# Zeros in the 11 unused columns of the values' stationary operand

## The chip, the core and the metric

The kernel runs on one core of one Trainium2 chip. The core has TensorE (PE in the profile; the loads of its stationary operand are listed apart as PEld), VectorE (DVE), ScalarE (ACT), GpSimd (POOL) and SyncE (SP), which mostly issues DMAs. The metric is the device time of one execution in microseconds, the median of several runs. About 0.2% (3.6 us) is what runs of this kernel can tell from no change.

## The reference

A gated sum of two branches over the same x of 2048 tokens by 640 channels, all in float32: 32-head attention with 20 channels a head, and a token-mixing MLP whose hidden width is 1728.

```python
def _A_ref(x, wqkv, wo):
    qkv = (lambda x, *d: x.transpose(*d))((x @ wqkv).reshape(B, S, 3, H, Dh), 2, 0, 3, 1, 4)
    q, k, v = qkv[0], qkv[1], qkv[2]
    scores = jnp.einsum("bhqd,bhkd->bhqk", q, k) * (Dh ** -0.5)
    p = _softmax(scores, axis=-1)
    o = jnp.einsum("bhqk,bhkd->bhqd", p, v)
    return (lambda x, *d: x.transpose(*d))(o, 0, 2, 1, 3).reshape(B, S, D) @ wo

def _B_ref(x, w1, b1, w2, b2):
    h = _layernorm(x, axis=-1)                                  # (B, S, D)
    u = _gelu(jnp.einsum("bsd,sf->bdf", h, w1) + b1)            # (B, D, F)
    y = jnp.einsum("bdf,fs->bds", u, w2) + b2                   # (B, D, S)
    return (lambda x, *d: x.transpose(*d))(y, 0, 2, 1)

g = _sigmoid((x * gate_w).sum(-1, keepdims=True))
return g * _A_ref(x, wqkv, wo) + (1 - g) * _B_ref(x, w1, b1, w2, b2)
```

(The reference's shapes: S = 2048, D = 640, H = 32, Dh = 20, F = 1728. The steps of gelu are written in one line here.)

## The kernel before

**Stages.** The program goes through these in order: the projections to queries and keys (`qk`, line 55), in the middle of them the projection to values (`v`, also line 55, called from lines 434 to 461); the MLP (`u` and `y`, line 49), with a first part of the score maxima (`s`, line 212) mixed in; the attention loop; and the output projection (`a`, line 1122). Products that must be exact to float32 are split into a high and a low part of the faster float32r type and done in three passes.

**The values.** For each half of the heads (16 heads) and each of the 16 token tiles t, 15 matmuls fill one PSUM tile with 128 tokens by 320 values. A POOL memset (line 454) writes ones in column 20 of each head in an SBUF tile `vt`, an ACT copy (line 455) brings the 320 values beside them, 21 columns a head, and one DMA on SP's queue (line 456) stores `vt` in the DRAM tensor `v_d`. `vt` has three buffers; the PSUM tiles of this stage go round four. In the second half of the heads ACT also squares a tile of x for the layer norm's statistics after each copy (line 432), and POOL issues the DMA that loads the tile of x four steps ahead (line 428). There the order of ACT, DVE and PE is as written; POOL's and SP's is set by the framework's scheduler up to the end of this stage, and as written behind it.

**The attention loop.** 16 pairs p of heads, and for each pair 32 iterations: two halves qh of 1024 queries by 16 tiles kt of 128 keys. One iteration g does:

- `st_pair` (line 1015): two matmuls of 512 queries, one a head, in the upper and lower 64 rows of the array, into the two banks of the PSUM tile `two`, which has a single buffer; then one ACT exponential of 1024 columns (line 1020) into an SBUF tile `pp` (three buffers).
- `st_one` (line 1023), twice: one matmul of 512 queries, then one ACT exponential of 512 columns (line 1028) into an SBUF tile `pt` (six buffers).
- between these, two matmuls `s` (line 212) for the score maxima of a later pair, each reduced by DVE (line 218); they run out 23 iterations before the end of the loop, where matmuls of the output projection of the first token tile take their place in most iterations.
- `pv_flush` (line 911): for the iteration before, four products of exponentials and values, one for each of two heads and two groups of 512 queries, in float32. Each fills 32 columns of the array (`pv[r: r + 32]`, r = 0, 32, 64, 96). The stationary operand is 32 columns of the values' tile `v`, of which 21 belong to the head: 20 values and the column of ones, whose result is the softmax's denominator.

In the profile each of the four `pv` products shows as two matmuls and two weight loads. Every 16 iterations the result is copied to SBUF (`pv_evac`, line 888) and stored.

**Where the 32 columns lie.** `v` holds for each key tile the 42 columns of a pair of heads, 21 and 21. Head 0 takes columns 0 to 31, so that its last 11 are the first 11 of head 1; head 1 takes columns 10 to 41, so that its first 11 are the last 11 of head 0. The results in those 22 rows of PSUM are never read: `pv_evac` picks rows `r` to `r + 20` for head 0, and 11 further for head 1. `load_v` (line 160) loads one pair's `v` from `v_d` while the pair before is worked on (iteration 13 of 32, line 1067); `v` has two buffers in the pool `base`. The first pair's is loaded in eight pieces during the MLP (line 814).

**Waits.** The framework gives each engine a semaphore and puts the waits into the instruction. An instruction that has to wait for two semaphores gets a separate semaphore instruction ahead of it in its engine's queue.

## Time and profile before

| what | value |
|---|---|
| time, median of 3 runs | 1786.04 us (1785.62 to 1786.98) |
| profiled execution | span 1786.8 us; the page gives no other time of its own for it |
| PE busy | 99% of the span, 15000 matmuls |
| ACT busy | 83% |
| DVE, POOL busy | 69%, 37% |
| the values' stage | 70.9 us, from 67.1 to 138.1 |
| the attention loop | 735 to 1708 us, 511 iterations with an exponential each and one whose exponentials are done before the loop |

A row of a timeline has the start and the duration in us, the engine, the line of the code, the operation, what it writes and reads, how many instructions were merged, and in brackets how long the engine had been idle before and what ended that. A busy PE is no PE at its peak, since the profile models the ends of pipelined matmuls: the share of 99% does not by itself say that PE sets the pace.

### The profile page before, as it was taken

What the parts mean: (1) busy time and instruction counts of PE and PEld (TensorE: products, weight loads), DVE (VectorE), ACT (ScalarE), POOL (GpSimd) and SP (SyncE); (2) the same over time, 40 slices, a digit from 0 to 9 for tenths busy, and PEclk for the clock granted to TensorE, in tenths of its full rate; (3) what the DMA queues carried; (4) which work ended last, traced back from release to release, by engine and by line L of the source; (5) the groups of instructions that cost most, each with busy time, mean ns of one, the idle gap of its engine ahead of it and who ended that gap; (6) DMA issues with size and microseconds to landing.
All of it is one profiled execution on the core that took longest, in us unless ns stands there. A gap on an engine that the chain in (4) does not pass through costs nothing.

```text
span 1786.8 us, 39925 instructions
## 1 busy us (share of the span) xinstructions
PE 1774.7 (99%) x15000; PEld 1106.2 (62%) x15000; DVE 1227.1 (69%) x2380; ACT 1483.3 (83%) x2534; POOL 654.3 (37%) x925
## 2 busy tenths in 40 slices
PE   9999999999999999999999999999999999999999
PEld 7998899999999999633333333333333333333378
DVE  5303288888888889776767676776777677767245
ACT  4244388888888886799999999999999999999930
POOL 1123578789877777211211111121322121212200
PEclk9999999999999999999999999999999999999999
DMA  8757876466675564335313224043353242301543
GB/s 280 251 167 241 268 182 167 142 182 200 176 191 146 160 173 150 82 72 119 63 31 86 54 64 96 10 110 66 49 136 70 46 94 57 74 13 47 195 132 134
DMA packets 155516, 222.34 MB, mean 124 GB/s; under 512 B 66420, under 2 KB 93444, under 8 KB 151640
## 3 DMA queue, kind: packets, MB, share of 16 engines
q1 hardware_dynamic: 136698, 188.82, 38.9%
q0 software_dynamic: 15888, 25.76, 6.0%
q10 hardware_dynamic: 2736, 5.21, 1.1%
q8 instruction: 118, 1.93, 0.5%
q14 instruction: 76, 0.62, 0.1%
HBM read 165.43 MB, written 53.92 MB: 123 GB/s over the span
## 4 chain that ended last, share of the span: by engine, by line
PE 96%; DMA 3%; DVE 0%; issue 0%; ACT 0%; POOL 0%; SPq 0%; DVEq 0%; ACTq 0%; POOLq 0%
PE pv L917 29%; PE st L1013 20%; PE s L212 13%; PE u L49 10%; PE y L49 10%; PE qk L55 7%; PE v L55 4%; PE a L1122 3%; DMA xr<-in_xT_dram 1%; DMA wr<-in_wqk_dram 1%; DMA rc_d<-rl_last 1%; DMA rbe<-r_d 0%; PE a L49 0%; DMA o_d<-oev 0%; DVE mx L218 0%
## 5 line engine op out<-in xcount | busy, mean ns | idle before, releaser
L218 DVE TENSOR_REDUCE mx<-s 128x1 f32<-128x512 f32 x1280 | 835.2, 687 | 285.7 <-PE s L212 214.3
L1028 ACT ACTIVATE p<-st 128x512 f32<-128x512 f32 x1022 | 567.5, 627 | 0.0
L917 PE MATMUL pv<-p,v 128*32 128x512 f32 x4088 | 546.8, 605 | 0.0
L1020 ACT ACTIVATE p<-st 128x1024 f32<-128x1024 f32 x511 | 536.8, 1051 | 2.6 <-PE s L212 1.8
L1013 PEld LDWEIGHTS st<-qs_True,ks_True 62*128 62x128 f32 x2044 | 245.3, 185 | 430.9 <-ACT p L1020 426.9
L1013 PE MATMUL st<-qs_True,ks_True 62*128 62x512 f32 x2044 | 495.5, 445 | 0.4 <-DVE ty L697 0.4
L212 PE MATMUL s<-ks_False,qs_False 60*128 60x512 f32 x1152 | 361.1, 394 | 0.1
L44 POOL TENSOR_TENSOR wl<-wr,wh 128x512 fp32r<-128x512 f32 x228 | 275.8, 1221 | 65.2 <-ACT wh L41 48.0
L237 DVE CUSTOM_DVE_ANT_0 ov<-s,ov 128x512 f32<-128x512 f32 x384 | 264.0, 688 | 38.0 <-PE s L212 25.9
L227 ACT ACTIVATE ov<-s 128x512 f32<-128x512 f32 x384 | 229.0, 598 | 65.1 <-PE s L212 54.6
L212 PE MATMUL s<-sk,sq 60*128 60x512 f32 x896 | 280.6, 394 | 0.0
L49 PE MATMUL y<-gh,wh 64*128 64x320 f32 x896 | 224.3, 307 | 0.0
L49 PE MATMUL y<-gl,wh 64*128 64x320 f32 x832 | 216.2, 306 | 0.0
L49 PE MATMUL y<-gh,wl 64*128 64x320 f32 x832 | 215.8, 305 | 0.0
L898 POOL DMA_DIRECT2D l_d<-oev x124 | 60.8, 497 | 410.4 <-DVE oev L890 402.1
L49 PE MATMUL u<-hh,wh 64*128 64x320 f32 x864 | 199.9, 307 | 0.0
L49 PE MATMUL u<-hl,wh 64*128 64x320 f32 x864 | 199.8, 307 | 0.0
L212 PEld LDWEIGHTS s<-ks_False,qs_False 60*128 60x128 f32 x1152 | 198.0, 185 | 2.4 <-DVE mx L218 0.4
L917 PEld LDWEIGHTS pv<-p,v 128*32 128x32 f32 x4088 | 82.3, 108 | 182.9 <-issue 169.9
L49 PE MATMUL u<-hh,wl 64*128 64x320 f32 x800 | 188.2, 307 | 0.0
L41 ACT ACTIVATE wh<-wr 128x512 fp32r<-128x512 f32 (+3 forms) x247 | 146.8, 598 | 37.7 <-PE y L49 13.3
L212 PEld LDWEIGHTS s<-sk,sq 60*128 60x128 f32 x896 | 166.1, 186 | 18.1 <-DVE mx L218 0.4
(148 smaller groups left out, 2388.2 us busy)
## 6 DMA issues: line engine op xcount, KB each, us to landing
wr<-in_w_dram SPq DMA_DIRECT2D x192, 256.0 KB
ks_True<-k_d SPq DMA_DIRECT2D x96, 160.0 KB
qs_True<-q_d SPq DMA_DIRECT2D x192, 80.0 KB
qs_False<-q_d SPq DMA_DIRECT2D x96, 80.0 KB
sk<-k_d SPq DMA_DIRECT2D x42, 160.0 KB
sq<-q_d SPq DMA_DIRECT2D x84, 80.0 KB
v_d<-vt SPq DMA_DIRECT2D x32, 168.0 KB
xr<-in_xT_dram SPq DMA_DIRECT2D x20, 256.0 KB
```

The lines of the kernel that those rows point to most:

```text
L41: nc.scalar.activation(hi, src, AF.Copy)
L44: (lo_eng or nc.vector).tensor_sub(lo, src, hi.bitcast(F32))
L49: nc.tensor.matmul(ps[k], a[r], b[r], start=start, stop=stop)
L55: nc.tensor.matmul(ps, a, b, start=(i == 0 and k == 0), stop=(i == n - 1 and k == 2))
L212: nc.tensor.matmul(ps, qs[half][r, t * P:(t + 1) * P], ks[r, kc * 512:(kc + 1) * 512], start=True, stop=True)
L218: nc.vector.tensor_reduce(mx[:, slot, j, t: t + 1], ps, axis=AX.X, op=OP.max)
L227: nc.scalar.activation(over[j, kc], ps, AF.Relu)
L237: nc.vector.tensor_tensor_reduce(ov, ps, ov, 1.0, -3.0e38, OP.add, OP.max, mx[:, slot, j, t: t + 1])
L917: nc.tensor.matmul(pv[r: r + 32, :], v_tiles[p][:, kt, 10 * j: 10 * j + 32], pt[j, c], start=(kt == 0), stop=(kt == NT - 1))
L1013: nc.tensor.matmul(ps, ks[r, kt * P:(kt + 1) * P], qs[qh][r, c * 512:(c + 1) * 512], start=True, stop=True)
L1020: nc.scalar.activation(pt, ps, AF.Exp, scale=SCALE)
L1028: nc.scalar.activation(pt, ps, AF.Exp, scale=SCALE)
```

## The change

The tile `v` becomes 53 columns wide for a pair of heads: 21 of head 0, 11 columns of zeros, 21 of head 1. Head 0 takes columns 0 to 31 as before (its 21, then the zeros), head 1 columns 21 to 52 (the zeros, then its 21), so that each head's results lie in the same rows of PSUM as before, and the 22 rows that are never read become zeros. In full:

```diff
-NPAIR = VW * 2
+NPAIR = 32 + VW
...
-    v_d = dram.tile([2, NT, P, 16 * VW], F32, name="v_d")
+    v_d = dram.tile([2, NT, P, 8 * NPAIR], F32, name="v_d")
...
     def load_v(p, pieces=1, put=nc.sync.dma_start):
-        v_tiles[p] = base.tile([P, NT, NPAIR], F32, tag="v", bufs=2, name=f"v{p}")
+        v_tiles[p] = (ap if p % 2 else base).tile([P, NT, NPAIR], F32, tag="v", bufs=1, name=f"v{p}")
         c0 = NPAIR * (p % 8)
...
-            vt = pvp.tile([P, 16, VW], F32, tag="vt", bufs=3, name=f"vt{half}_{t}")
-            nc.gpsimd.memset(vt[:, :, DH], 1.0)
-            nc.scalar.activation(vt[:, :, :DH], ps[:, :HALF].rearrange("p (h w) -> p h w", w=DH), AF.Copy)
+            vt = pvp.tile([P, 8, NPAIR], F32, tag="vt", bufs=3, name=f"vt{half}_{t}")
+            nc.gpsimd.memset(vt[:, :, VW: 32], 0.0)
+            for j in range(2):
+                nc.gpsimd.memset(vt[:, :, 32 * j + DH], 1.0)
+                nc.scalar.activation(vt[:, :, 32 * j: 32 * j + DH], ps[:, :HALF].rearrange("p (h j w) -> p h j w", j=2, w=DH)[:, :, j], AF.Copy)
             nc.sync.dma_start(v_d[half, t], vt.rearrange("p h w -> p (h w)"))
...
-                    nc.tensor.matmul(pv[r: r + 32, :], v_tiles[p][:, kt, 10 * j: 10 * j + 32], pt[j, c],
+                    nc.tensor.matmul(pv[r: r + 32, :], v_tiles[p][:, kt, VW * j: VW * j + 32], pt[j, c],
                                      start=(kt == 0), stop=(kt == NT - 1))
...
-        pt = lp.tile([P, 512], F32, tag="pt", bufs=6, name=f"p{g}_1{j}")
+        pt = lp.tile([P, 512], F32, tag="pt", bufs=5, name=f"p{g}_1{j}")
```

So for each of the 32 tiles `vt`, three memsets stand in place of one and two ACT copies of 160 values in place of one of 320; a store has 212 KB in place of 168, and a load of `v` 424 KB in place of 336. The two buffers of `v` now lie in two pools, `base` for even and `ap` for odd pairs, and `pt` has five buffers in place of six.

The waits move too, which the diff does not show. The first place is ACT in the attention loop, iterations 37 and 38. In a row, `p37_0` is the exponential of `st_pair`, `p37_10` and `p37_11` those of the two `st_one`; the brackets name the semaphores that are waited for (`PE_49` is PE's, `Activation_49` ACT's own). Before:

```order
L1020 ACTIVATE p37_0_14441<-st37_0_14438 128x1024 [waits PE_49,Activation_49]
L1028 ACTIVATE p37_10_14445<-st37_10_14443 128x512 [waits PE_49,Activation_49]
L1028 ACTIVATE p37_11_14455<-st37_11_14453 128x512 [waits PE_49]
L1020 ACTIVATE p38_0_14487<-st38_0_14484 128x1024 [waits PE_49,Activation_49]
L1028 ACTIVATE p38_10_14491<-st38_10_14489 128x512 [waits PE_49,Activation_49]
L1028 ACTIVATE p38_11_14501<-st38_11_14499 128x512 [waits PE_49]
```

And with the change:

```order
L1022 ACTIVATE p37_0_14537<-st37_0_14534 128x1024 [waits PE_49]
L1030 ACTIVATE p37_10_14541<-st37_10_14539 128x512 [waits PE_49,Activation_49]
L1030 ACTIVATE p37_11_14551<-st37_11_14549 128x512 [waits PE_49]
L1022 ACTIVATE p38_0_14583<-st38_0_14580 128x1024 [waits PE_49]
L1030 ACTIVATE p38_10_14587<-st38_10_14585 128x512 [waits PE_49,Activation_49]
L1030 ACTIVATE p38_11_14597<-st38_11_14595 128x512 [waits PE_49]
```

The wide exponential no longer waits for ACT's own semaphore, so that it needs no semaphore instruction ahead of it; this is so in 508 of the 511 iterations. PE's order in the loop and its waits are as before.

The second place is POOL in the second half of the values' stage, tiles 3 to 6 (`vt1_3` and so on; `xn` are the tiles of x; `DMAHW` waits are for the store that frees the buffer). Before:

```order
L454 MEMSET vt1_3_1150 128x16 [waits DMAHW2_49,Pool_49]
L428 DMA xn5_1109<-in_x_dram 128x640 [waits DMASW1_49,Activation_49]
L454 MEMSET vt1_4_1173 128x16 [waits DMAHW3_49,Pool_49]
L428 DMA xn6_1132<-in_x_dram 128x640 [waits DMASW2_49,Activation_49]
L454 MEMSET vt1_5_1196 128x16 [waits DMAHW4_49,Pool_49]
```

And with the change:

```order
L428 DMA xn5_1163<-in_x_dram 128x640 [waits DMASW1_49,Activation_49]
L454 MEMSET vt1_4_1233 128x8x11 [waits DMAHW3_49,Pool_49]
L456 MEMSET vt1_4_1233 128x8 x2
L428 DMA xn6_1189<-in_x_dram 128x640 [waits DMASW2_49,Activation_49]
L454 MEMSET vt1_5_1259 128x8x11 [waits DMAHW4_49,Pool_49]
L456 MEMSET vt1_5_1259 128x8 x2
```

Each memset has become three, at the same place between the DMAs. Beside this, 12 of the second half's 16 value tiles and the four `qk` tiles behind them get a second wait on their first matmul, for PE's own semaphore, and so do DVE's 16 small copies of the gate's columns (line 458), so that PE and DVE each have 16 semaphore instructions more. PE's waits are for a matmul three tiles back.

## The prediction

> **What bounds the kernel now.** I read the chain of waits first, then the clock by stage, then single iterations of the attention loop. The chain's shares and its three longest pieces:
>
> ```profile
> PE pv L917 29%; PE st L1013 20%; PE s L212 13%; PE u L49 10%; PE y L49 10%; PE qk L55 7%; PE v L55 4%; PE a L1122 3%; DMA xr<-in_xT_dram 1%; DMA wr<-in_wqk_dram 1%; DMA rc_d<-rl_last 1%; DMA rbe<-r_d 0%; PE a L49 0%; DMA o_d<-oev 0%; DVE mx L218 0%
> ...
> 34.00 33.13 PE qk L55 x137
> 67.13 70.92 PE v L55 x480
> 138.05 84.00 PE qk L55 x360
> ```
>
> The chain is PE nearly throughout. The change touches two stages: the values' stage, 480 matmuls without a break in 70.92 us, and the attention loop, whose `pv`, `st` and `s` are 62% of the chain. PE's modelled ends would hide a wait, so the loop has to be checked by starts. First its pace, as the wide exponential, one an iteration, shows it in the part with the `s` matmuls (738 to 1663 us) and in the part after they have run out; the columns are the stretch, its length, ACT's busy time in this line with the count, the granted TensorE clock, the DMA share and GB/s:
>
> ```profile
> 738.00:1663.00 925.00, 508.92 (x487) 1.00 0.32 69
> 1663.00:1707.00 44.00, 26.42 (x23) 1.00 0.57 196
> ```
>
> 925.00 / 487 = 1.899 us an iteration with `s`, 44.00 / 23 = 1.913 without. PE has less to do in the second part and is not faster: there something else sets the pace. Two stretches of the timeline, one of each part (start, duration, in brackets the idle time ahead):
>
> ```profile
> 1041.85 1.04 ACT L1020 ACTIVATE p<-st 128x1024 f32<-128x1024 f32 x1
> 1042.15 1.07 PE L917 MATMUL pv<-p,v 128*32 128x512 f32 x8
> 1042.77 1.09 ACT L1028 ACTIVATE p<-st 128x512 f32<-128x512 f32 x2
> 1043.14 0.29 PEld L1013 LDWEIGHTS st<-qs_True,ks_True 62*128 62x128 f32 x3 [0.84 <-ACT p L1020]
> 1043.74 1.04 ACT L1020 ACTIVATE p<-st 128x1024 f32<-128x1024 f32 x1
> 1044.04 1.07 PE L917 MATMUL pv<-p,v 128*32 128x512 f32 x8
> 1045.04 0.29 PEld L1013 LDWEIGHTS st<-qs_True,ks_True 62*128 62x128 f32 x3 [0.84 <-ACT p L1020]
> 1045.64 1.04 ACT L1020 ACTIVATE p<-st 128x1024 f32<-128x1024 f32 x1
> ```
>
> ```profile
> 1665.24 1.05 ACT L1020 ACTIVATE p<-st 128x1024 f32<-128x1024 f32 x1
> 1665.37 1.11 PE L917 MATMUL pv<-p,v 128*32 128x512 f32 x8
> 1666.41 0.19 PEld L1013 LDWEIGHTS st<-qs_True,ks_True 62*128 62x128 f32 x2 [0.84 <-ACT p L1020]
> 1667.11 1.09 ACT L1020 ACTIVATE p<-st 128x1024 f32<-128x1024 f32 x1
> 1668.31 0.19 PEld L1013 LDWEIGHTS st<-qs_True,ks_True 62*128 62x128 f32 x2 [0.84 <-ACT p L1020]
> 1668.96 1.13 ACT L1020 ACTIVATE p<-st 128x1024 f32<-128x1024 f32 x1
> ```
>
> The next `st` may load only when the wide exponential has emptied the single PSUM tile `two`. Without `s` the exponential ends at 1667.11 + 1.09 = 1668.20 and the load follows at 1668.31, 0.11 later: ACT comes last. With `s` it ends at 1043.74 + 1.04 = 1044.78 and the load comes at 1045.04, 0.26 later. If 0.11 is enough, 0.15 us of ACT's lead goes unused and PE comes last, whatever the bracket names: the load follows the eight `pv` matmuls after 0.99 (1042.15 to 1043.14) and 1.00 us (1044.04 to 1045.04).
>
> ACT is close behind. Without `s` the wide exponentials start 1.87 and 1.85 us apart (1665.24, 1667.11, 1668.96), but their durations grow from 1.05 to 1.13, so that they end at 1666.29, 1668.20 and 1670.09, 1.91 and 1.89 apart. Starting earlier only lengthens the time in ACT's pipe. So ACT's own pace is about 1.90 us too. PE and ACT are balanced to a hundredth of a microsecond, and a gain needs both.
>
> [...]
>
> **The change, part by part.**
>
> *The loop's matmuls.* Nothing is added or removed: four products of 32 columns, with other addresses and zeros in 22 of 64 columns.
>
> ```profile
> L917 PEld LDWEIGHTS pv<-p,v x4088: 105/108/111, 737.9 to 1707.2; 128*32 128x32 f32 x195
> L917 PE MATMUL pv<-p,v x4088: 592/604/618, 737.9 to 1707.6; 128*32 128x512 f32 x195
> ```
>
> Their durations (least, median, most) do not depend on the values so far as the trace can show: 4088 loads of different data lie within 6 ns. For the zeros I take 0, bounded by the clock, which is granted at 1.00 in both parts, so that nothing is left to gain. For the addresses the trace has loads that start every 8 bytes (steps of 168 and 40 bytes) and none at an odd multiple of 4 (212 and 84 bytes now). The bounds: no gain, and as a loss one spread, 111 - 105 = 6 ns, on each of an iteration's eight loads if all lie on PE's path, 8 x 0.006 x 511 = 24.5 us. I take 0, since the loads that are there, at many alignments, differ by so little.
>
> *The wide exponential's semaphore instruction.* It goes in 508 of 511 iterations:
>
> ```profile
> L1020 ACTq EVENT_SEMAPHORE  x509: 17/17/17, 734.7 to 1704.9; - x170
> ```
>
> That is 17 ns each, 8.6 us of ACT's queue. What it can be worth lies between 0 and the difference of the pace now and the closest starts seen: 1.899 - 1.86 (the mean of 1.87 and 1.85) = 0.04 us an iteration, 487 x 0.04 = 19 us. I take 0 in the 487 iterations with `s`, because PE comes last there, 0.15 us behind ACT, and would not see it. Without this cover ACT's ends, 1.90 us apart, would still hold it. In the 23 iterations at the end, where ACT is last, the same 0.04 would be 0.9 us at most; I take a third, -0.3 us, since the ends speak against more.
>
> *`pt` with five buffers.* The exponential 2g + 1 of iteration g now overwrites the one five before, that of iteration g - 2. Its readers, `pv` of g - 2, stand on PE ahead of `st` of g, whose result the exponential needs anyway. So no later wait: 0. If it did come later, ACT would wait for PE, which is last already, so that it would show in full.
>
> *The values' stage.* What is added lies on ACT, POOL and the queues:
>
> ```profile
> L454 POOL MEMSET vt<- x32: 128/132/152, 47.4 to 134.1; 128x16 f32 x32
> L455 ACT ACTIVATE vt<-v x32: 420/439/441, 72.5 to 138.2; 128x320 f32<-128x320 f32 x32
> ...
> L1028 ACT ACTIVATE p<-st 128x512 f32<-128x512 f32 x1022 | 567.5, 627 | 0.0
> L1020 ACT ACTIVATE p<-st 128x1024 f32<-128x1024 f32 x511 | 536.8, 1051 | 2.6 <-PE s L212 1.8
> L44 POOL TENSOR_TENSOR wl<-wr,wh 128x512 fp32r<-128x512 f32 x228 | 275.8, 1221 | 65.2 <-ACT wh L41 48.0
> ```
>
> ACT: (1051 - 627) / 512 = 0.83 ns a column, so a copy of 160 takes about 439 - 133 = 306 ns, two 612: +0.17 us a tile; bounds +0 (the same columns) and +0.44 (the full 439 again). POOL: two more memsets, each at least 132 ns, the one of 88 columns at most 132 + 88 x 1221 / 512 = 342: +0.26 to +0.47 us a tile, I take 0.35. The stores: 44 KB more each, at the 180 GB/s that the cell of this stage shows below 0.25 us. What hides it:
>
> ```profile
> 67.00:138.00 71.00, 71.00 (x482) 71.00 (x481) 8.84 (x28) 29.13 (x69) 12.41 (x45) 1.00 0.56 180
> ...
> 107.42 0.44 ACT L455 ACTIVATE vt<-v 128x320 f32<-128x320 f32 x1 [0.95 <-PE v L55]
> 109.63 0.44 ACT L455 ACTIVATE vt<-v 128x320 f32<-128x320 f32 x1 [0.96 <-PE v L55]
> 110.49 0.13 POOL L454 MEMSET vt<- 128x16 f32 x1 [0.98 <-DMA v_d<-vt]
> 114.03 0.44 ACT L455 ACTIVATE vt<-v 128x320 f32<-128x320 f32 x1 [0.96 <-PE v L55]
> ```
>
> The first row has PE, PEld, DVE, ACT and POOL: PE is full, ACT works 29 of 71 us, POOL 12. A tile takes 109.63 - 107.42 = 2.21 us, and ACT waits 0.96 of that for PE; 0.17, even 0.44, fits in. The copy at 107.42 fills a buffer, its store lands and the memset at 110.49 frees it for the third copy after, at 114.03: 114.03 - 110.62 = 3.41 us to spare, against 0.35 + 0.25 + 0.17 = 0.77 added. And PE itself goes round four PSUM tiles, so that a copy that ends 0.17 later is still some three tiles, 6.6 us, early. The stage costs 0. Queued behind POOL's memsets are the loads of `xn`, needed four tiles later: 0. If the spare 3.41 us were gone, each further 0.1 us a buffer would cost up to 0.1 x 32 / 3 = 1 us.
>
> *16 semaphore instructions on PE and 16 on DVE.* PE's wait for a matmul that is three tiles old. The nearest row is `L917 PEldq EVENT_SEMAPHORE` at 51 ns:
>
> ```profile
> L917 PEldq EVENT_SEMAPHORE  x19: 51/51/51, 737.4 to 1647.7; - x19
> ```
>
> Between 0 and 16 x 0.051 = 0.8 us; I take 0, as PE's loads run ahead of its matmuls in this stage (71.00 us busy). DVE is busy 8.84 of 71 us there: 0.
>
> *The loads of `v`.* 424 KB each in place of 336, issued on SP's queue 19 iterations, 19 x 1.899 = 36 us, before the pair starts. DMA is busy 0.32 of the loop: 0.
>
> **Sum:** 0 in the values' stage, 0 in 487 iterations, -0.3 us in the last 23. The profiled execution's span is 1786.8 us, 0.8 above the median of the three runs and inside what they span, so the sum is set on the median: 1786.04 - 0.3 = 1785.7 us.
>
> **Rivals.**
>
> *ACT was the one that set the pace, and its shorter queue speeds up the loop.* For it: the two engines lie within 0.01 us, and the profile names ACT as what `st` waits for. Against it: the 0.26 us between ACT's end and the load where 0.11 is enough, and ends 1.90 us apart where ACT does come last. It would give up to 487 x 0.04 + 0.9 = 20 us, so 1766 to 1782 us.
>
> *The weight loads at 4-byte offsets are slower.* It is one mechanism, on PE in every iteration, and it decides from 3.6 / 511 = 7 ns an iteration on, since PE comes last with nothing to spare. For it: no such address is in the trace. Against it: 6 ns over all the others. At 8 x 6 ns the time is 1785.7 + 24.5 = 1810 us; at the smallest that can be told 1789.3.
>
> *The values' stage gets bound by the round of `vt`'s buffers.* Needs more than 3.41 us where 0.77 is added; at 1 us more a buffer, 11 us and 1797 us.
>
> *Zeros let TensorE run at a higher clock.* The clock's column shows 1.00 in the loop, which leaves nothing there. Over the whole span the core's row is
>
> ```profile
> core 0: 1786.8 us, clock 0.998
> ```
>
> This 0.998 could give 0.2%, 1786.04 x 0.002 = 3.6 us, 1782.5 us, if the gap lay under `pv`, which the 1.00 there excludes. [...]
>
> **How the numbers follow.** Hidden everywhere 0.86; ACT's queue 0.05; slower loads 0.05; `vt`'s round 0.02; the clock 0.02. 0.2% (3.6 us) is about what a measurement of this kernel can tell from no change. Faster: 0.05 + 0.02 = 0.07; within: 0.86; slower: 0.05 + 0.02 = 0.07. The range is the likeliest case's own, which holds more than 8 in 10: below it the rest of the 0.9 us of the last iterations (0.6), the scatter of the runs (1786.98 - 1785.62 = 1.4 us) and 0.7 of what ACT's queue could be worth give 1783; above it the 0.8 us of PE's semaphores, that scatter and 1.6 of the loads' bound give 1789.5.
>
> **What would show it.** Right: 1.90 us between wide exponentials in both parts, with `st` loaded about 0.26 us after ACT's end with `s` (or a little more, as ACT starts sooner); `pv` loads at 108 and matmuls at 604 ns; 480 matmuls in 70.9 us; about 508 semaphore instructions of ACT gone. Wrong: a loop that takes another time than 970 us, `pv` loads above 111 ns, a break in PE's `v` matmuls, or ACT waiting for the store of `vt`.

## The result, and the profile after

The changed kernel takes **1778.33 us** (median of 5 runs, 1777.0 to 1779.45) where the kernel before, beside it, takes 1786.12 (1785.62 to 1789.53): a ratio of **0.9947, 95% interval 0.9935 to 0.996**. The prediction was 1785.7 us in a range from 1783.0 to 1789.5, with 0.07 on faster. It was wrong: the kernel is faster by 0.5%, 7.8 us.

First the places that the prediction named. The profile of the changed kernel, by lines: the semaphore instruction of the wide exponential, the loads and matmuls of `pv`, the three memsets and copies of the values' tile (least, median and most ns, first and last start):

```profile
L1022 ACTq EVENT_SEMAPHORE  x1: 17/17/17, 727.3 to 727.3; - x1
L919 PEld LDWEIGHTS pv<-p,v x4088: 105/108/111, 730.1 to 1698.0; 128*32 128x32 f32 x195
L919 PE MATMUL pv<-p,v x4088: 592/604/618, 730.1 to 1698.4; 128*32 128x512 f32 x195
L454 POOL MEMSET vt<- x32: 175/177/195, 46.1 to 133.2; 128x88 f32 x32
L456 POOL MEMSET vt<- x64: 113/115/134, 46.2 to 133.6; 128x8 f32 x64
L457 ACT ACTIVATE vt<-v x64: 290/308/340, 71.8 to 136.1; 128x160 f32<-128x160 f32 x64
```

The loads of `pv` have the same three durations as before, 105/108/111 ns, with zeros and at 4-byte offsets; the matmuls too. The semaphore instruction is gone but for one. A copy of 160 columns takes 308 ns (306 forecast), the memsets together 177 + 2 x 115 = 407 ns, 0.28 us more a tile than the 132 of before (0.35 forecast). The values' stage, in the chain of waits, takes the time it took:

```profile
64.80 70.89 PE v L55 x480
```

70.89 us against 70.92, though it starts 2.3 us earlier (64.80 against 67.13). And in the loop the wide exponential's pace (stretch, length, ACT's busy time in this line, granted clock, DMA share, GB/s) and one wide exponential with the load of `st` behind it:

```profile
731.00:1656.00 925.00, 504.66 (x487) 1.00 0.32 70
```

```profile
1041.03 1.04 ACT L1022 ACTIVATE p<-st 128x1024 f32<-128x1024 f32 x1
...
1042.38 0.29 PEld L1015 LDWEIGHTS st<-qs_True,ks_True 62*128 62x128 f32 x3 [0.84 <-ACT p L1022]
```

487 iterations still fill 925 us; the load comes at 1042.38, 0.31 us behind ACT's end at 1042.07, where it came 0.26 behind. ACT runs earlier, and PE doesn't follow as far as this count can tell, which is in whole iterations of 1.9 us.

So the parts of the change do what was forecast, or nearly. Most of the time went in stages that no edit touches. The busy time of PE in `qk` after the values' stage (the stretch from 100 to 420 us, 360 matmuls), and in the two passes of the up-projection `u` (0 to 420 and 420 to 700 us, 1312 matmuls each). Before:

```profile
100.00:420.00 320.00, 84.16 (x360) 1.00 0.67 197
...
0.00:420.00 420.00, 129.56 (x1312) 1.00 0.68 208
420.00:700.00 280.00, 130.60 (x1312) 1.00 0.63 171
```

After:

```profile
100.00:420.00 320.00, 82.58 (x360) 1.00 0.69 202
...
0.00:420.00 420.00, 128.13 (x1312) 1.00 0.71 214
420.00:700.00 280.00, 128.43 (x1312) 1.00 0.64 171
```

With the clock at 1.00 in each row: -1.58 us in `qk`, -1.43 and -2.17 in `u`. The loop, by the first and last start of `pv`, went from 1707.6 - 737.9 = 969.7 to 1698.4 - 730.1 = 968.3 us, -1.4. Together -6.6 of the 7.8 us. The start (67.13 to 64.80) and the end behind the last `pv` (1786.8 - 1707.6 = 79.2, 1775.2 - 1698.4 = 76.8) give 4.7 us more between these two profiles, but they differ as much between executions of one kernel, as the first experiment shows.

How the matmuls of `qk` got faster is seen in the ns between the starts of neighbours, from the 101st matmul of that stage on:

```
before   234 233 233 234 233 233
after    225 230 231 226 229 232
```

PE waits for nothing in either: the profile has no idle time ahead of any of the 360. It runs an even rhythm of 233.3 ns before and an uneven one of 229 after. The experiments ask what chooses the rhythm, and whether the edits of the change have any part in it.

### The profile page after: what moved, and what is told of

Same layout as the page of the kernel before. It is cut to its first block, busy times and chain, and to the rows that moved or that the text cites. A ratio compares the mean times of both kernels' runs of the same rounds, so it can differ in the third digit from the quotient of the medians.

```text
span 1775.2 us, 39545 instructions
## 1 busy us (share of the span) xinstructions
PE 1765.1 (99%) x15000; PEld 1091.8 (62%) x15000; DVE 1225.5 (69%) x2380; ACT 1483.9 (84%) x2566; POOL 658.3 (37%) x989
## 2 busy tenths in 40 slices
DMA packets 155513, 225.20 MB, mean 127 GB/s; under 512 B 66420, under 2 KB 93444, under 8 KB 151640
## 4 chain that ended last, share of the span: by engine, by line
PE 95%; DMA 3%; DVE 1%; issue 0%; POOL 0%; ACT 0%; SPq 0%; DVEq 0%; ACTq 0%; POOLq 0%
PE pv L919 29%; PE st L1015 22%; PE s L212 12%; PE y L49 10%; PE u L49 9%; PE qk L55 6%; PE v L55 4%; PE a L1124 2%; DMA wr<-in_wqk_dram 1%; DMA xr<-in_xT_dram 1%; DMA rbe<-r_d 0%; DMA rc_d<-rl_last 0%; DMA k_d<-evh 0%; DVE oy L1130 0%; PE a L49 0%
## 5 line engine op out<-in xcount | busy, mean ns | idle before, releaser
L212 PEld LDWEIGHTS s<-ks_False,qs_False 60*128 60x128 f32 x1152 | 210.4, 184 | 3.0 <-ACT ov L227 0.8
L49 PE MATMUL u<-hh,wh 64*128 64x320 f32 x864 | 206.9, 304 | 0.0
L49 PE MATMUL u<-hl,wh 64*128 64x320 f32 x864 | 206.7, 304 | 0.0
L49 PE MATMUL u<-hh,wl 64*128 64x320 f32 x800 | 194.4, 304 | 0.0
```

The source lines that it names most:

```text
L49: nc.tensor.matmul(ps[k], a[r], b[r], start=start, stop=stop)
L212: nc.tensor.matmul(ps, qs[half][r, t * P:(t + 1) * P], ks[r, kc * 512:(kc + 1) * 512], start=True, stop=True)
```

## The experiments

Stage lengths in the expectations are counted from the first start of a stage to the first of the next; the rows below give busy time, which differs from it by up to 1 us. All numbers of one kind are compared with their own kind.

### The same two kernels once more

No edit, and one run each.

> The kernel before, unchanged, for a second profile. Between the two profiles so far (before, after) the stages differ thus, in us: first qk stage 61.4 to 59.1, second qk stage (360 matmuls) 84.1 to 82.5, u of the first half 129.7 to 128.3, u of the second half 130.3 to 128.1, attention loop 971.6 to 970.2, output projection 78.6 to 76.3; v and y within 0.4. Theory 'cadence' (PE falls into one of several steady rhythms in qk and u, and the program decides into which): the second qk stage is 84.1 and the u stages about 130 again, and only the first qk stage and the output projection may move. Theory 'scatter' (an execution falls into a rhythm by chance): qk and u may come out at 82.5 and 128 here.

> The changed kernel, unchanged, for a second profile. 'Cadence': second qk stage 82.5, u 128.3 and 128.1, loop 970.2 again. 'Scatter': they may come out at 84.1 and 130. The first qk stage (59.1) and the output projection (76.3) may move by 2 us under both, as they begin and end with single transfers.

Measured: 1784.82 and 1779.04 us. The kernel before, in the chain of waits of its second profile:

```profile
63.49 70.92 PE v L55 x480
```

and the busy time of `qk` there:

```profile
100.00:420.00 320.00, 84.16 (x360) 1.00 0.67 197
```

The values' stage starts at 63.49 where it started at 67.13: the start of the program, which waits for loads, moves by 3.6 us from one execution to the next, the last stage by some us too. `qk` is again 84.16 us, and 82.58 in both profiles of the changed kernel. From the values' stage on the stages' lengths belong to the program (the second `u` has 130.37 us here and 130.60 in the first profile), the start and the end to the execution.

### The two parts that the prediction had costed: `pt` and the copies

Five `pt` buffers alone, which also takes ACT's semaphore instructions away:

```diff
-        pt = lp.tile([P, 512], F32, tag="pt", bufs=6, name=f"p{g}_1{j}")
+        pt = lp.tile([P, 512], F32, tag="pt", bufs=5, name=f"p{g}_1{j}")
```

> The kernel before with pt in five buffers and nothing else of the change: ACT loses the 508 semaphore instructions of the wide exponential; PE's queue is that of before. 'ACT's queue' (the gain comes from these): about 1778 us, ratio 0.995. 'Cadence by PE's own 16 extra semaphore instructions': loop 1 to 1.5 us shorter at most, second qk stage 84.1, u 130: about 1785 us, ratio 0.999. 'Zeros' or 'addresses': 1786 us, ratio 1.000.

Two copies for each values tile alone, which also gives PE its 16 waits:

```diff
-            nc.scalar.activation(vt[:, :, :DH], ps[:, :HALF].rearrange("p (h w) -> p h w", w=DH), AF.Copy)
+            for j in range(2):
+                nc.scalar.activation(vt.rearrange("p (h j) w -> p h j w", j=2)[:, :, j, :DH], ps[:, :HALF].rearrange("p (h j w) -> p h j w", j=2, w=DH)[:, :, j], AF.Copy)
```

> The kernel before with the ACT copy of the values in two (even and odd heads of each pair), the layout of 21 columns a head, the values, the memsets and pt as before: PE and DVE get the same 16 semaphore instructions more as in the change, ACT's queue in the loop is that of before. 'Cadence by PE's 16 extra semaphore instructions': second qk stage 82.5 in place of 84.1, u 128 in place of 130, together -5 us: about 1781 us, ratio 0.997. 'ACT's queue', 'zeros', 'addresses': 1786 us, ratio 1.000.

Measured: `pt5` 0.9997 (0.9987 to 1.0007), `split` 0.9988 (0.998 to 0.9997). The rows of `pt5` for ACT's semaphore instructions in the line of the wide exponential, and for the matmuls of `pv`:

```profile
L1020 ACTq EVENT_SEMAPHORE  x1: 17/17/17, 732.4 to 732.4; - x1
```

```profile
L917 PE MATMUL pv<-p,v x4088: 592/604/618, 735.6 to 1704.5; 128*32 128x512 f32 x195
```

The instructions are gone and the loop is 968.9 us, 0.8 shorter. By the starts of the wide exponentials, the part with `s` went from 925.82 to 925.09 us and the last 22 periods from 41.58 to 41.52. So five buffers and the loss of 508 instructions of 17 ns, 8.6 us of queue, are together worth 0.8 us: ACT isn't the one that sets the pace. Five buffers also move tiles of the loop (`pt`, `sq`, `sk`) by multiples of 2048 bytes; no run separates that from the instructions. `split` has `qk` at 84.16 us and the second `u` at 130.59, as before: PE's extra waits don't choose the rhythm.

### Something else than zeros

```diff
-            nc.gpsimd.memset(vt[:, :, VW: 32], 0.0)
+            nc.gpsimd.memset(vt[:, :, VW: 32], 0.37)
```

> The changed kernel with 0.37 in the place of zero in the 11 unused columns of the values' stationary operand: rows of the product that nobody reads hold other numbers, all else is as changed. Theory 'zeros' (less switching in TensorE's array): the time returns to about 1786, the loop to 971.6 us. Theory 'addresses': 1778.5 us as the changed kernel, the loop at 970.3, the second stage of queries and keys at 82.50, the up-projections at 128.

Measured: 0.9947 (0.9935 to 0.9958). Its core's span and clock, and its matmuls of `pv`:

```profile
core 0: 1777.4 us, clock 0.998
```

```profile
L919 PE MATMUL pv<-p,v x4088: 592/604/618, 728.8 to 1697.2; 128*32 128x512 f32 x195
```

The same ratio as with zeros, to the last digit, and a loop of 968.4 us. What the change is named after has no effect on the time that these runs can tell.

### Nothing but the places of tiles

Tiles are laid out one behind the other in each partition of SBUF, and pools on top of pools, so that the size of one tile moves those that are allocated with it. In the changed kernel the three buffers of `vt` are 352 bytes larger each, and what lies above them stays: they start 352, 704 and 1056 bytes lower, and the values' weights `wv` below them in that pool 3 x 352 = 1056, with `wvr`, from which they are split. The pool `base` holds one tile `v` of 16 x 53 columns in place of two of 16 x 42: 2 x 2688 - 3392 = 1984 bytes less, and the tiles of the up-projection, `hh` and `hl` with the `xm`, `ov` and `ty` beside them, lie 1984 bytes lower. Tiles of the loop and of the output projection move too. The operands of `qk` and the weights of `u` stay where they were.

The kernel before with larger `vt` tiles, of which no more is used than before:

```diff
-            vt = pvp.tile([P, 16, VW], F32, tag="vt", bufs=3, name=f"vt{half}_{t}")
+            vt = pvp.tile([P, 8 * 53], F32, tag="vt", bufs=3, name=f"vt{half}_{t}")[:, :16 * VW].rearrange("p (h w) -> p h w", w=VW)
```

> The kernel before, with each values tile `vt` given 424 columns of which the same 336 are used: no instruction, transfer or value differs, but the values' weights `wv`, which are allocated behind these tiles, stand 1056 bytes lower, as in the changed kernel. Theory 'addresses of wv' (the place of the values' weights sets the rhythm in which TensorE takes its matmuls, and the next stage goes on in it): the second scores stage for the queries and keys falls from 84.09 to 82.50 us, the values' stage ends at 70.9 us with its matmuls no longer at an even 147 ns, and the time falls by 1.6 us or more, to about 1784. Theory 'addresses of hh and hl' (only the operands of the up-projection count): the second stage of queries and keys stays at 84.09 us, the up-projections at 130 us, the time at 1786. Theory 'zeros' (the zeros in the weights of the loop make the change): nothing changes, 1786.

The kernel before with `v` allocated 53 wide in two pools, 42 columns used, and five `pt`:

```diff
-        v_tiles[p] = base.tile([P, NT, NPAIR], F32, tag="v", bufs=2, name=f"v{p}")
+        v_tiles[p] = (ap if p % 2 else base).tile([P, NT, 53], F32, tag="v", bufs=1, name=f"v{p}")[:, :, :NPAIR]
...
-        pt = lp.tile([P, 512], F32, tag="pt", bufs=6, name=f"p{g}_1{j}")
+        pt = lp.tile([P, 512], F32, tag="pt", bufs=5, name=f"p{g}_1{j}")
```

> The kernel before with five buffers of `pt` and with the two buffers of the loop's values `v` given 53 columns of which the same 42 are used, in two pools as in the changed kernel: no instruction or value differs from the kernel with five buffers of `pt` (1786.1 us), but the tiles behind them stand where the changed kernel has them: `hh` and `hl`, the moving operands of the up-projection, 1984 bytes lower, and the tiles of the attention loop. `wv` stays where the kernel before has it. Theory 'addresses of hh and hl': both up-projections fall from 130 to 128 us, the second stage of queries and keys stays at 84.09, the time falls by 3 to 4 us, to about 1782.5. Theory 'addresses of wv': the second stage of queries and keys stays at 84.09 us and the up-projections at 130, the time at 1786. Theory 'zeros': 1786.

Both edits:

> The kernel before with both of these edits: all tiles stand where the changed kernel has them, and nothing else of the change is there (no zeros, one copy of 320 columns for each values tile, the same transfers, the 10-column steps of the weights). Theory 'addresses' in any form: the second stage of queries and keys 82.50 us, the up-projections 128 us, the loop 970.3 us, the time about 1779, a ratio of 0.995 to 0.996. Theory 'zeros' and theory 'copies and transfers of the values': stages as before, 1786, a ratio of 0.999 to 1.0.

Measured: `vt_wide` 0.9997 (0.9989 to 1.0006), `v_wide` 0.9965 (0.9952 to 0.9978), `places` 0.9968 (0.9956 to 0.998). The rows of `qk` and of the two passes of `u`, and the one of `pv`. In `vt_wide`:

```profile
100.00:420.00 320.00, 82.58 (x360) 1.00 0.68 197
...
0.00:420.00 420.00, 129.67 (x1312) 0.99 0.69 209
420.00:700.00 280.00, 130.59 (x1312) 1.00 0.63 170
```

In `v_wide`:

```profile
100.00:420.00 320.00, 84.16 (x360) 1.00 0.69 197
...
0.00:420.00 420.00, 127.95 (x1312) 1.00 0.70 209
420.00:700.00 280.00, 128.44 (x1312) 1.00 0.64 171
```

```profile
L917 PE MATMUL pv<-p,v x4088: 592/604/618, 733.0 to 1701.2; 128*32 128x512 f32 x195
```

And in `places`:

```profile
100.00:420.00 320.00, 82.58 (x360) 1.00 0.68 199
...
0.00:420.00 420.00, 128.05 (x1312) 1.00 0.70 210
420.00:700.00 280.00, 128.45 (x1312) 1.00 0.64 171
```

This settles where the time went. Each pad moves one stage and leaves the other, and both together give the stages of the changed kernel: 82.58, 128.05 and 128.45 us, against 82.58, 128.13 and 128.43. Not one instruction of `vt_wide` does anything else than in the kernel before. `vt_wide`'s 1.58 us are 0.09% of the time, which its interval holds and cannot tell from nothing; `v_wide`'s 0.35%, 6.3 us, can be told. The loop of `v_wide` is 968.2 us, 0.7 below that of `pt5`, which is what the moved tiles of the loop give.

That `qk` gains from `vt_wide` is odd, since none of its own operands moved. But PE goes from the last `v` matmul to the first of `qk` without a break (145 ns from start to start in the kernel before, 147 in the changed one). With the old places `v` ends in an even rhythm (starts 147, 147, 146 ns apart, over and over), with the new ones in an uneven one (148, 145, 148, 145, 149); `qk` then goes on evenly or unevenly too. (A kernel further down, `grid1`, breaks this: there `v` is uneven and `qk` even.)

The first part of `qk`, ahead of `v`, runs unevenly in nearly all profiles, of the kernel before too. Not so in two. From the 201st matmul of that part on:

```
before  226 229 232 225 230 231
v_wide  233 234 233 233 234 233
```

In `v_wide` this part is even from its 17th matmul to its end, and in `grid2`, further down, for its first 100, though `v_wide` moves no tile that is in use before `u`. At 4.4 ns a matmul (233.3 - 228.9) that is 1 us in the profile of `v_wide`. So in this part, where PE starts and stops with the loads (in the kernel before it is idle ahead of 3 of the 240 matmuls, 1.9 us in all), the rhythm can differ with none of its tiles moved; what is said of places rests on the second part and on `u`.

### Which places

First the changed kernel with all of its edits and pads that bring `wv` and `hh`, `hl` to multiples of 128 bytes from their old places:

```diff
-            vt = pvp.tile([P, 8, NPAIR], F32, tag="vt", bufs=3, name=f"vt{half}_{t}")
+            vt = pvp.tile([P, 8, NPAIR + 1], F32, tag="vt", bufs=3, name=f"vt{half}_{t}").rearrange("p h w -> p (h w)")[:, :8 * NPAIR].rearrange("p (h w) -> p h w", w=NPAIR)
...
-        v_tiles[p] = (ap if p % 2 else base).tile([P, NT, NPAIR], F32, tag="v", bufs=1, name=f"v{p}")
+        v_tiles[p] = (ap if p % 2 else base).tile([P, NT * NPAIR + 16], F32, tag="v", bufs=1, name=f"v{p}")[:, :NT * NPAIR].rearrange("p (k w) -> p k w", w=NPAIR)
```

> The changed kernel with all of its edits, zeros included, and two pads that nobody reads or writes: 8 columns behind each values tile `vt` (it moves `wv` down by 96 bytes, to 1152 below its place in the kernel before) and 16 columns behind each loop tile `v` (it moves `hh`, `hl` up by 64 bytes, to 1920 below their place in the kernel before). 1152 and 1920 are multiples of 128, so that these operands stand against a grid of 128 bytes (and of 64) as in the kernel before, though at other addresses. Theory 'place on a grid of 128 bytes': the change's gain goes where the zeros stay: second stage of queries and keys 84.09 us, up-projections 130 us each, time up by 5 to 6 us over the changed kernel's, to 1783 to 1785. Theory 'distance' (it is how far apart tiles lie, or which part of the memory they are in, that counts): 82.50 and 128 us, 1778.5. Theory 'the change's own edits': 1778.5.

And the kernel before with small pads, 8 columns behind each `vt` and each `v`:

```diff
-            vt = pvp.tile([P, 16, VW], F32, tag="vt", bufs=3, name=f"vt{half}_{t}")
+            vt = pvp.tile([P, 16 * VW + 8], F32, tag="vt", bufs=3, name=f"vt{half}_{t}")[:, :16 * VW].rearrange("p (h w) -> p h w", w=VW)
...
-        v_tiles[p] = base.tile([P, NT, NPAIR], F32, tag="v", bufs=2, name=f"v{p}")
+        v_tiles[p] = base.tile([P, NT * NPAIR + 8], F32, tag="v", bufs=2, name=f"v{p}")[:, :NT * NPAIR].rearrange("p (k w) -> p k w", w=NPAIR)
```

> The kernel before (six buffers of `pt`, one copy for each values tile, no zeros) with pads of 8 columns behind each `vt` and behind each loop tile `v`: `wv` 96 bytes lower, `hh` and `hl` 64 bytes higher than before, everything else in place. Against a grid of 64 bytes `wv` stands as in the changed kernel, against one of 128 it stands otherwise than in both; `hh` and `hl` stand on both grids as in the changed kernel. Theory 'place on a grid': up-projections 128 us each; second stage of queries and keys 82.50 us if 64 bytes are its grid, 84.09 or a third value if it is 128; the loop 971.6 us as before if its gain came with five `pt` and the moved tiles of the loop; together 1780.5 to 1782. Theory 'distance': 130 and 84.09 us, 1786.

Measured: `undo` 0.9959 (0.9944 to 0.9974), `shift_small` 0.9965 (0.9952 to 0.9977). In `undo`:

```profile
100.00:420.00 320.00, 82.58 (x360) 1.00 0.69 200
...
0.00:420.00 420.00, 128.97 (x1312) 1.00 0.70 213
420.00:700.00 280.00, 129.21 (x1312) 1.00 0.62 171
```

In `shift_small`:

```profile
0.00:420.00 420.00, 127.95 (x1312) 0.99 0.69 209
420.00:700.00 280.00, 128.47 (x1312) 1.00 0.63 172
```

`undo` speaks against a grid of 128 bytes for `wv`: it stands on it as before, and `qk` is fast. For `hh` and `hl` it says half: 129.21 is between 130.60 and 128.43. `shift_small` shows that 96 bytes are enough for `qk` (82.58 too) and 64 for `u`: distance plays no part. Four more kernels, with one run each and pads of other sizes in the same two lines: 16, 32, 64 and 128 columns behind `vt`; 8 or 24 behind one `v`, 16 behind both, or `v` in two pools (`grid4`, with six `pt`; the others have five). The one of `grid1`:

```diff
-            vt = pvp.tile([P, 16, VW], F32, tag="vt", bufs=3, name=f"vt{half}_{t}")
+            vt = pvp.tile([P, 16 * VW + 16], F32, tag="vt", bufs=3, name=f"vt{half}_{t}")[:, :16 * VW].rearrange("p (h w) -> p h w", w=VW)
...
-        v_tiles[p] = base.tile([P, NT, NPAIR], F32, tag="v", bufs=2, name=f"v{p}")
+        v_tiles[p] = base.tile([P, NT * NPAIR + 8 * (p % 2)], F32, tag=f"v{p % 2}", bufs=1, name=f"v{p}")[:, :NT * NPAIR].rearrange("p (k w) -> p k w", w=NPAIR)
```

> The kernel before with five `pt` buffers and pads: `wv` 192 bytes lower (a multiple of 64, not of 128), `hh` and `hl` 32 bytes higher. Theory 'grid of 128': second stage of queries and keys off 84.09 us (82.50), up-projections faster than 130 us unless only 64 of 128 is a fast place. Theory 'one unlucky place': 82.50 and about 128 us. One look: about 1781 us if both are fast, 1786 if both are slow.

> The kernel before with five `pt` buffers and pads: `wv` 384 bytes lower (three times 128), `hh` and `hl` 96 bytes higher. Theory 'grid of 128': second stage of queries and keys 84.09 us; up-projections as in the run with 32 bytes. Theory 'one unlucky place': 82.50 and about 128 us. One look: about 1783 us by the first, 1781 by the second.

> The kernel before with five `pt` buffers and pads: `wv` 768 bytes lower (six times 128), `hh` and `hl` 128 bytes higher. Theory 'grid of 128': second stage of queries and keys 84.09 us and up-projections 129.4 to 130 us, about 1785. Theory 'one unlucky place': 82.50 and 128 us, about 1781.

> The kernel before with its two loop tiles `v` in two pools (`hh` and `hl` 2688 bytes lower, 21 times 128; six `pt` buffers) and `wv` 1536 bytes lower (12 times 128). Theory 'grid of 128': second stage of queries and keys 84.09 us, up-projections 129.4 to 130 us, about 1785. Theory 'one unlucky place': 82.50 and 128 us, about 1781.

Measured: 1784.0, 1783.75, 1782.96 and 1782.26 us, against 1784.55 of the kernel before on that chip; only the stages are read from them. In `grid2`, where `wv` lies 384 bytes lower, and in `grid3`, where it lies 768 lower:

```profile
100.00:420.00 320.00, 82.58 (x360) 1.00 0.68 199
```

```profile
100.00:420.00 320.00, 84.16 (x360) 1.00 0.68 198
```

All kernels by how far the operands were moved, in bytes, with the rest on division by 256 in brackets, and the busy time of the stage in us:

| kernel | `wv` moved | `qk` | `hh`, `hl` moved | second `u` |
|---|---|---|---|---|
| before | 0 (0) | 84.16 | 0 (0) | 130.60 |
| `grid3` | -768 (0) | 84.16 | +128 (128) | 129.34 |
| `grid4` | -1536 (0) | 84.16 | -2688 (128) | 129.32 |
| `grid1` | -192 (64) | 84.16 | +32 (32) | 129.38 |
| `undo` | -1152 (128) | 82.58 | -1920 (128) | 129.21 |
| `grid2` | -384 (128) | 82.58 | +96 (96) | 129.41 |
| `shift_small` | -96 (160) | 82.58 | +64 (64) | 128.47 |
| after, `places` | -1056 (224) | 82.58 | -1984 (64) | 128.43, 128.45 |
| `v_wide` | 0 (0) | 84.16 | -1984 (64) | 128.44 |
| `vt_wide` | -1056 (224) | 82.58 | 0 (0) | 130.59 |

Both theories that went into these runs fall. One unlucky place is out, since `qk` is slow at four places of `wv`; a grid of 128 bytes is out, since -384 and -1152 are fast. What fits all rows is that the place counts modulo 256 bytes: `qk` is slow at 0 and 64 and fast at 128, 160 and 224, without a third value; `u` has three values, slow at 0, fast at 64, between them at 32, 96 and 128. The rhythm of the `v` matmuls says the same more finely. The ns between starts, from the 302nd matmul on:

```
before  (0)    147 146 147 147 146 147 147 146
grid3   (0)    146 147 147 146 147 147 146 147
grid4   (0)    147 147 146 147 147 146 147 147
grid1   (64)   145 149 146 150 143 145 149 146
undo    (128)  144 146 150 147 143 146 150 148
grid2   (128)  144 146 150 147 143 146 150 148
shift_s (160)  146 147 146 148 145 148 146 147
vt_wide (224)  149 145 148 145 148 145 149 145
```

(`shift_s` is `shift_small`.) Kernels with the same rest have the same rhythm, though their operands lie hundreds of bytes apart. `grid1` shows that a stage doesn't simply hand its rhythm on: its `v` is as uneven as that of the fast kernels, and its `qk` runs at an even 233.3 ns. That 256 is the period was formed from these rows and not tried on new ones; it is the least power of two that fits, and 512 contradicts no row of the table either.

### What is left: the copies

Two kernels with two copies a values tile, `split` and `fill`, lay 1.3 and 4.0 us below `pt5` and `places`, which have one copy and ran beside them. First the other way: the changed kernel with one copy for both heads, from tiles of 64 columns a pair, with a store that picks 53:

```diff
-            vt = pvp.tile([P, 8, NPAIR], F32, tag="vt", bufs=3, name=f"vt{half}_{t}")
+            vt = pvp.tile([P, 8, 64], F32, tag="vt", bufs=3, name=f"vt{half}_{t}")
             nc.gpsimd.memset(vt[:, :, VW: 32], 0.0)
-            for j in range(2):
-                nc.gpsimd.memset(vt[:, :, 32 * j + DH], 1.0)
-                nc.scalar.activation(vt[:, :, 32 * j: 32 * j + DH], ps[:, :HALF].rearrange("p (h j w) -> p h j w", j=2, w=DH)[:, :, j], AF.Copy)
-            nc.sync.dma_start(v_d[half, t], vt.rearrange("p h w -> p (h w)"))
+            vj = vt.rearrange("p h (j w) -> p h j w", j=2)
+            nc.gpsimd.memset(vj[:, :, :, DH], 1.0)
+            nc.scalar.activation(vj[:, :, :, :DH], ps[:, :HALF].rearrange("p (h j w) -> p h j w", j=2, w=DH), AF.Copy)
+            nc.sync.dma_start(v_d[half, t].rearrange("p (h w) -> p h w", w=NPAIR), vt[:, :, :NPAIR])
```

> The changed kernel with its values tiles 64 columns wide for a pair of heads, so that one copy and one ones-fill on GpSimd serve both heads, and the 53 columns are picked by the store; the zeros are left out (11 columns hold what was there). `hh` and `hl` stand as in the changed kernel, `wv` 2112 bytes lower than before (a multiple of 64, not of 128). Theory 'place on a grid': up-projections 128 us each, the loop 970.3; second stage of queries and keys 84.09 us if 64 bytes are its grid, perhaps 82.50 if 128. Theory 'copies': 2 us more in the start and the end than the changed kernel, so 1781 to 1782.5; if the copies do nothing, 1778.5 to 1780.

(The expectation is wrong in one point: as the diff shows, the zeros are written in this kernel too.)

Measured: 1.0256 (1.0241 to 1.0272), 1834.29 against 1789.17 us, 45 slower, which neither theory had. A piece of the chain of waits; the stretch of the values' stage (PE, PEld, DVE, ACT and POOL, then clock, DMA share and GB/s), of this kernel and of the changed one; and the page's line on DMA packets, of this kernel and of the one before:

```profile
71.53 14.10 DMA v_d<-vt
85.65 0.04 ACTq L457
85.69 0.04 issue
85.73 0.45 ACT vt L457
86.23 9.16 DMA v_d<-vt
```

```profile
66.00:179.00 113.00, 82.84 (x476) 76.50 (x475) 7.72 (x26) 25.91 (x62) 14.18 (x67) 0.92 1.03 113
```

```profile
64.80:135.70 70.90, 70.90 (x481) 70.87 (x481) 9.09 (x28) 31.06 (x100) 16.70 (x104) 1.00 0.63 206
```

```profile
DMA packets 184184, 225.19 MB, mean 123 GB/s; under 512 B 99188, under 2 KB 122116, under 8 KB 180312
```

```profile
DMA packets 155516, 222.34 MB, mean 124 GB/s; under 512 B 66420, under 2 KB 93444, under 8 KB 151640
```

The store leaves SBUF in eight pieces of 53 x 4 = 212 bytes a partition in place of one of 1696. The kernel has 99188 packets under 512 bytes where the kernel before and the changed one have 66420, 32768 = 32 stores x 128 x 8 more. The DMA engines are full (1.03) at 113 GB/s, the copies wait 9 to 14 us for a store to free their buffer, and the stage takes some 42 us more. This is the round of `vt`'s buffers that the prediction had among its rivals, brought on by the form of the store and not by its size. The changed kernel's stage, with as many bytes to store, moves 206 GB/s at a share of 0.63. `u` was 128.46 in its second pass, as at the other places with rest 64.

Then `places` with the two copies of `split`:

> The kernel before with all tiles where the changed kernel has them (as in `places`, 0.9968 of the time before) and ScalarE's copy of each values tile in two, as in `split` (0.9988). It is the changed kernel without zeros, without larger transfers. Theory 'copies' (the two copies are worth the 2 us that `split` showed, in addition): a ratio of 0.9947 as the changed kernel. Theory 'scatter' (start and end differ from execution to execution, and the copies do nothing): 0.9965 as `places`.

Measured: 0.9949 (0.9936 to 0.9963), as the theory 'copies' had it. Both partners once more on one chip:

> `places` once more: one copy for each values tile. Both theories: a ratio of 0.9965 of the time before.

> `places_split` once more: two copies for each values tile, all else as in `places`. Theory 'copies': a ratio of 0.9948, 3 us below `places`, of which the stretch from the second gate stage to the first `pv` matmul shows 0.35 us (126.4 against 126.7). Theory 'scatter': the same as `places` within 1 us.

Measured: 0.9955 (0.9944 to 0.9967) and 0.9952 (0.9939 to 0.9965), medians 1779.88 and 1779.24 us: 0.6 us apart, where the theory 'copies' asked for 3. The difference between the two pairs is scatter, or most of it. What the profiles show of the copies is about 0.35 us, from the start of the second pass of `y` to the first `pv` (126.6 to 126.7 us with one copy, 126.2 to 126.4 with two); why it shows there is open.

Without zeros, larger stores, 4-byte offsets and further memsets, `places_split` has the changed kernel's time, 0.9949 and 0.9952 against 0.9947. No version tried beats it by more than can be measured.

## Why the prediction was wrong, point by point

- **What bounds the kernel:** right. PE comes last in the loop: `st` loads 0.26 us behind ACT's end before and 0.31 after, where 0.11 is enough in the iterations without `s`. ACT's queue as the pace setter, a rival with 0.05, is out: `pt5` takes the instructions away for 0.8 us, not 19.
- **The loop's matmuls, 0:** right for what was costed. Loads of 105/108/111 ns and matmuls of 592/604/618 are unchanged at 4-byte offsets, and the bound of +24.5 us was empty.
- **The wide exponential's semaphore instruction, 0 with `s` and -0.3 at the end:** a size off, on the wrong side of the loop. `pt5` shows -0.7 us in the part with `s` and -0.06 in the last 22 periods. PE gained 1.5 ns an iteration where 0 was forecast, from ACT's earlier start or from the tiles that five buffers move.
- **The values' stage, the waits, the loads of `v`, 0:** right, 70.89 against 70.92 us; the copy as forecast, the memsets (+0.28 us a tile) below it (+0.35).
- **The zeros and the clock, 0.02:** the gain is about twice what this rival gave (3.6 us), but not by it: `fill` has the same time without a zero (0.9947, at a clock of 0.998).
- **The step that failed is the sum.** It has a term for each edit and none for the stages between them, as if a stage without an edit had the time it had. The sizes of `vt` and `v` are edits of every tile that is laid out behind them, and the prediction used the addresses for one operand only, the 32 columns of `v`. It had `qk` at 84.00 and `u` in the chain's shares on its first rows and read nothing from them. Worth: `qk` -1.58, `u` -1.43 and -2.17, the moved tiles of the loop -0.6 (what `pt5` leaves of the loop's -1.4; `shift_small`, with six buffers, has a loop 0.7 shorter than before) and `pt` with its semaphores -0.8 us, -6.6 together; 0.35 with the copies; what is left of 7.8 us, about 0.9, is within what the start and the end scatter by.
- **The range** was too narrow for the same reason. No row of the profile before bounds this: all of them have the tiles in one place.

The sign could not have been forecast from the profile before. That the layout moves could have been: it follows from the sizes in the diff.

## What to carry to other kernels

Here a change of two tiles' sizes moved what is allocated behind them (`wv` by 1056 bytes, `hh` and `hl` by 1984), and PE's time in an untouched stage changed by 2% for that alone (84.16 against 82.58 us in `qk`, `vt_wide`), so stages that no edit touches belong in the comparison, and in the range. Before a gain or a loss of half a per cent is put down to an edit, run the old code with only the sizes of the new one (`places`): here that control had most of the gain (0.9968 and 0.9955, against 0.9947). Where such a stage is long, pads of a few columns are worth trying: 64 bytes gave 3.7 us in `u` (`shift_small`).

## What the runs showed of the hardware that was not expected

- A stage of back-to-back matmuls on PE can run in more than one steady rhythm (233.3 or 229 ns a matmul in `qk`; three busy times in the second pass of `u`, 130.4 to 130.6, 129.2 to 129.4 and 128.4 to 128.5 us), at a granted clock of 1.00. In the second part of `qk` and in `u`, which one it takes goes with the address of SBUF tiles in all rows of the table and in the kernels outside it: `pt5` and `split`, with the old places, have 84.16 and 130.59 us, `fill` and `places_split`, with the new ones, 82.57 and 128.44 or 128.46 (but `qk` of `after_one`, in which PE waits 4.0 us for copies behind the values' stores, has 88.04 us at a clock of 0.97). In the first part of `qk` it differed with no tile moved that is in use there (`v_wide`), so the address isn't all that decides.
- The cause behind it is open. Which tile counts is not settled either: the three buffers of `vt` and `wvr` move with `wv`, and `xm`, `ov` and `ty` with `hh` and `hl`; no run moved one without the others. The tiles moved here all start at multiples of 32 bytes, and the runs show that among these there is a difference in time (84.16 against 82.58 us in `qk`, 130.60 against 128.43 in the second pass of `u`). No run here tests whether the rhythm has to do with another engine's accesses.
- Without the 17 ns of semaphore instruction on ACT in each iteration, and with ACT's end 0.26 us ahead, PE's iteration is 1.5 ns shorter (`pt5`; that the five buffers' places have no part in it is not shown).
